# One converted weight per two units in the second gated pass, and four re-ordered stretches around it

## The chip, the cores and the metric
The kernel runs on one core of one Trainium2 chip. The metric is the time of one execution on the device in microseconds (us): lower is better. Three runs of the kernel before gave 1425.16 us as their median (1423.47 to 1425.9). Differences of under 0.2% (some 2.9 us) can't be told from none here.

## The reference, cut to what matters
Eight batches and eight heads of an attention between 512 tokens and 32 state rows (64 wide), read both ways, then a gated layer over the 4352 rows, then a second layer with a piecewise quadratic activation. All is float32.

```python
# attention, per batch and head: x is 512x64, state is 32x64
a     = softmax(scale * x @ state.T);   xread = a @ state      # 512x64
a2    = softmax(scale * state @ x.T);   sread = a2 @ x         # 32x64
x = concat(xread, sread) over rows, heads side by side -> (8*544, 512)
# layer 1 (w_gate, w_val 512x1536; w_out 1536x512)
x = (sigmoid(x @ w_gate) * (x @ w_val)) @ w_out
# layer 2 (w_in 512x2048; w_out 2048x512): g is 0, (h+1)^2/4 or h by where h lies
h = x @ w_in
out = where(h >= 1, h, where(h <= -1, 0, (h+1)**2/4)) @ w_out
```

## The kernel before, in words
Each float32 product is made of three products of shortened halves (high times high, high times low, low times high), so every operand is split: ScalarE (ACT) copies the high half, VectorE (DVE) subtracts it to get the low half. The program is one long order written out by hand: each engine works through its own queue in order, and a wait at the head of a queue holds all that is behind it. SyncE (SP) issues nearly all DMAs, in order as well.

The stages, in order of time:

- **First attention** (0 to 50 us), for batches 0 to 3, order in the string `PRE`. Each word is a step with a number: `X` transposes x on TensorE (PE) and ACT copies it; `st`/`sb` do that for the state; `S` scores, `E` their copy, `A` their transpose, `m` maximum and subtraction on DVE, `x` exp on ACT, `n` normalisation (`att_n`), `T` transpose with the high half on ACT, `L` the low half on DVE; `p` and `j` (`Weights.parts`, `Weights.join`) convert one weight tile, two instructions on ACT, then two on DVE; `M` multiplies a pair of weights by the state (PE, then the high half on ACT), `K` is its low half on DVE; `Q` begins the first gated products. In `att_n` the sum over 32 columns is made by halving adds on GpSimd (POOL), two small DVE instructions follow, and POOL multiplies. 14 transposes of the identity run ahead of the first data (L1366).
- **First gated pass** `gated(0)` (to 215 us), 24 units, a unit being 24 products of 128x512.
- **First output pass** `output1(0)` (to 378 us): 24 units of four slots each (`slot1(n, k)`, n from 0 to 95); a slot is six products of 128x512. The second half's attention and the state-side reads are items placed at slot numbers by hand: `t_item` (T of the second half) at 36, 38, 58, 60, `att_n` of the last head pair at 56, `sr_e` (a maximum on DVE, two exps on ACT, then five small DVE instructions) at 49, 51, 53, 55 for the second half, `sr_items` at 62 to 88. At slot 70 four weight tiles `wa` are loaded.
- **Second gated pass** `gated(1)` (to 543 us). In each unit PE does half of its products, `prev()` evacuates the unit before (two sigmoids on ACT, L658, or two multiplies on DVE, L661), one pair of `m_item` may follow, then `split_ws` splits a weight tile into a two-buffered tile `w` and stores it, and `parts`/`join` convert weights for layer 2; an even unit has two rounds of `split_ws` and `parts`, an odd one two joins. `more_wa` loads the next `wa` tiles as far as splits and products allow. `m_pair` of an odd unit needs the PSUM tiles that the two sigmoids empty.
- **Second output pass** `output1(1)` (to 734 us), again slots (`slot2`). From slot 0 on, every second slot does one step of `wi_steps`, which load, combine, split and store the eight weight blocks of layer 2; the state rows `xs` are split at slot 5; at slot 71 the four loads of the third `ws` block are issued, out of space that the steps' tiles held. After slot 71 `state_block` does layer 1 for the state rows, then the slots 72 to 95 take one step each of the list `early`: four loads of y, four loads of weights, sums, high and low halves.
- **Layer 2** (to the end), with its steps planned at tick numbers. `to_last` plans the first operands of the last products.

The lines that decide are these, of `gated`:

```python
else:                                # bg == 1
    for _ in range(2):
        if i % 2 == 0 or i == 1:
            split_ws()
        if i % 2 == 0:
            if len(weights.first) < 2:
                weights.parts()
        elif i > 1:
            weights.join()
```

Of the kernel before, what the change touches and what calls it, by code (L numbers as in the profile page):

```python
# [25 lines left out]
def attention_moe_moe_kernel(  # L26
# [28 lines left out]
    nc = tc.nc  # L55
# [277 lines left out]
        t = t_of(bg, hp)  # L333
        nc.scalar.activation(out=t, in_=t, func=AF.Exp, scale=SCALE)

    def att_n(bg, hp, eng=None):
        t = t_of(bg, hp)
        u = att.tile([128, 16, 2, 1], F32, tag="u", name="u", bufs=2)
        if eng:
            v = att.tile([128, 16, 2, N // 2], F32, tag="v", name="v", bufs=1)  # L340
            n = N // 2
            src = t
            while n:
                o = v[:, :, :, :n] if n > 1 else u
                eng.tensor_tensor(
                    out=o, in0=src[:, :, :, :n], in1=src[:, :, :, n : 2 * n], op=ALU.add
                )
                src, n = v, n // 2
        else:
            nc.vector.tensor_reduce(out=u, in_=t, axis=AX.X, op=ALU.add)  # L350
        nc.vector.tensor_scalar(out=u, in0=u, scalar1=1e-9, scalar2=None, op0=ALU.add)
        nc.vector.reciprocal(out=u, in_=u)
        (eng or nc.vector).tensor_tensor(
            out=t, in0=t, in1=u.to_broadcast([128, 16, 2, N]), op=ALU.mult
        )
# [242 lines left out]
    def gated(bg, begun=None, hooks={}):  # L598


        sg_t = {}
        prev = None
        for i in range(4 * NQ):
            q, mm, v = i // 4, i // 2 % 2, i % 2
            if i == 0 and begun:
                ps = begun
            else:
                ps = [ps_tile(v) for _ in range(2)]
                if i == 0:
                    quads(ps, bg, q, mm, v, [((0,), 0)])  # L610
                    for _ in range(2):
                        m_item(1)
                    quads(ps, bg, q, mm, v, [((0,), 1)])
                    split_ws()
                else:
                    quads(ps, bg, q, mm, v, [((0, 1), 0)])
                if prev:
                    prev()
                if (i in (2, 3) or i > 4 and i % 2) if bg else i % 2:
                    for _ in range(2):  # L620
                        if m_done[bg] < 4 * NQ:
                            m_item(1 - v)
            if bg == 0:
                flush()
                weights.low()
                weights.high()
                weights.join()
                weights.load()
                weights.parts()
                if i % 2 == 0 and i < 18:  # L630
                    weights.parts()
                    weights.join()
            else:
                for _ in range(2):
                    if i % 2 == 0 or i == 1:
                        split_ws()
                    if i % 2 == 0:
                        if len(weights.first) < 2:
                            weights.parts()
                    elif i > 1:  # L640
                        weights.join()
            flush()
            weights.load()
            if i in hooks:
                hooks[i]()
            if i:
                quads(ps, bg, q, mm, v, [((0, 1), 1)])
            elif not begun:
                quads(ps, bg, q, mm, v, [((1,), 0), ((1,), 1)])
            if bg:  # L650
                more_wa()

            def evac(q=q, mm=mm, v=v, ps=ps):
                m = 2 * q + mm
                for t in range(2):
                    if v == 0:
                        sg_t[t] = sgp.tile([128, 2, 512], F32, tag="sg", name="sg", bufs=4)
                        nc.scalar.activation(out=sg_t[t], in_=ps[t], func=AF.Sigmoid)  # L658
                    else:
                        sg = sg_t[t]  # L660
                        nc.vector.tensor_tensor(out=sg, in0=sg, in1=ps[t], op=ALU.mult)  # L661
                        stores.append(
                            lambda sg=sg, t=t: nc.sync.dma_start(
                                out=h_dram[bg][:, m, 2 * t : 2 * t + 2], in_=sg
                            )
                        )

            prev = evac
        prev()
        flush()  # L670
# [621 lines left out]
    def combine(j, b, k, acc, cs, ev):  # L1292
# [55 lines left out]


    PRE = (  # L1350
# [3 lines left out]
    ).split()  # L1354
    st_r = load_state(0, nc.sync)
    weights.todo += [job_m(i) for i in range(8)]
# [6 lines left out]
    weights.load(1)  # L1363
    make_identity(nc, ident)
    warm = ps_tile(1)
    for i in range(14):  # L1366
        nc.tensor.transpose(warm[:, i % 2, :128], ident, ident)
    nc.vector.memset(half, 0.5)
    for b in range(4):
# [7 lines left out]
    for w in PRE:  # L1377
# [18 lines left out]
        elif c == "E":  # L1396
            att_e(0, n)
        elif c == "n":
            att_n(0, n, nc.gpsimd)
        elif c == "T":  # L1400
            att_t(0, n // 2, n % 2, 1)
        elif c == "L":
# [127 lines left out]
    for i, n in enumerate((18, 28, 40, 50)):  # L1530
        place(n, s_item(i))
        place(n + 2, a_item(i))
    for i, n in enumerate((36, 38, 58, 60)):
        place(n, t_item(i // 2, i % 2))
    place(56, lambda k: att_n(1, HP - 1))
    for i, n in enumerate((5, 7, 13, 21)):
        place(n, lambda k, i=i: sr_e(0, i))
    for i, n in enumerate((49, 51, 53, 55)):
        place(n, lambda k, i=i: sr_e(1, i))
    for f, n in zip(sr_items(0), (11, 13, 15, 17, 19, 21, 23, 27, 29, 31, 33, 35, 37)):  # L1540
        place(n, f)
    for f, n in zip(sr_items(1), (62, 64, 66, 68, 70, 74, 76, 78, 80, 82, 84, 86, 88)):
        place(n, f)

    def slot1(n, k):
# [21 lines left out]
            weights.slot()  # L1567
        if n == 90:
            m_item(k)
        if n == 94:  # L1570
            nc.scalar.activation(out=table, in_=half, func=AF.Sigmoid)

# [14 lines left out]
    mp = pool("mp1", side="right", stack=st_a)  # L1587
    sgp = pool("sgp1", side="right", stack=st_a)
    m_item(0)
    gated(1, None, {14: lambda: load_h(4, 0), 18: lambda: load_h(4, 1)})  # L1590
    while wsq:
        split_ws()
# [26 lines left out]
    early, lows = [], []  # L1619

    def slot2(n, k):
        if n == 5:
            nc.scalar.activation(out=xs_hi, in_=f32(xs_lo), func=AF.Copy)
            tt(nc.vector, xs_lo, f32(xs_lo), f32(xs_hi))
        if 8 <= n < 72 and n % 8 == 0:
            load_ws((n - 8) // 32, (n - 8) // 8 % 4)
        if n < 70:
            if n % 2 == 0 and wi_steps:
                wi_steps.pop(0)()
        elif n == 70:  # L1630
            st_g.close()
            wsps.append(pool("wsp2", stack=st_g))
        elif n < 72:
            for j in range(4):
                load_ws(2, j)
        elif early:
            early.pop(0)()

    def state_block(b):
# [28 lines left out]
        h3 = splits_y(0, range(7), nc.vector)[:3]  # L1668
        yh = [lambda f=f: lows.append(f()) for f in h3]
        yl = lambda: lows.pop(0)()  # L1670
        early.extend([*loads, *ld[:3], sums[0], ld[3], sums[1], wh[0], wl[0], sums[2], wh[1]])
        early.extend([wl[1], sums[3], wh[2], wl[2], wh[3], wl[3], yh[0]])
        early.extend([lambda: (yh[1](), yl()), lambda: (yh[2](), yl()), yl])

    output1(1, slot2, state_block)
# [108 lines left out]
    def to_last():  # L1784
# [2 lines left out]
        htp = pool("htp", side="right")  # L1787
        S0 = prep_h(0)
        for i, f in enumerate(f for s in sorted(S0) for f in S0[s]):
            plan(start[9] + 3 + 2 * i // 3, f)  # L1790

    plan(start[9], to_last)
    t = 0
# [67 lines left out]
```

## Time and profile before

| what | value |
|---|---|
| median of three runs | 1425.16 us |
| the profiled execution itself | 1424.11 us |
| its span, first to last instruction | 1422.3 us |
| PE busy | 1377.1 us, 97% |
| DVE, ACT, POOL busy | 889.9, 741.9, 278.6 us |
| mean granted clock of PE | 0.992 |
| mean DMA rate | 221 GB/s |

PE is busy nearly all the time. The 45.2 us in which it is not, and the stretches in which its granted clock is at the lower of its two levels (1.2 in place of 2.4 GHz), are what an order of instructions can change. A granted clock of 1.00 is the upper level, 0.50 the lower.

### The profile page before, as it was taken

Reading aid. Unit: us, or ns where it says so; the run is one execution under the profiler, and the core shown is the slowest. Engines: PE = TensorE matmul, PEld = TensorE weight load, DVE = VectorE, ACT = ScalarE, POOL = GpSimd, SP = SyncE. Lnnn points to the kernel's source line nnn. Section 1 sums busy time; section 2 is a strip of 40 time slices with the busy share of each in tenths; the row PEclk is TensorE's granted clock in tenths of the full one; section 3 lists DMA queues with packets and bytes.
Section 4 is the critical chain, followed back from the end, with each engine's and each line's share of the span. In section 5 each row is a group of like instructions: output and inputs, shape, how many; then the busy total and the mean of one; then the engine's idle time right before and its main releaser. Section 6 shows DMA issues by size and latency. Waiting matters only on the chain. (4 is left out here: it accounts for less than half of the span.)

```text
span 1422.3 us, 23220 instructions
## 1 busy us (share of the span) xinstructions
PE 1377.1 (97%) x9022; PEld 1166.6 (82%) x9022; DVE 889.9 (63%) x1289; ACT 741.9 (52%) x1097; POOL 278.6 (20%) x179
## 2 busy tenths in 40 slices
PE   7899999989989999999999999999999999999997
PEld 5677787777756677889978888878879999999997
DVE  5766566585356544542286665666578978787775
ACT  6655556564444432322267777787775434343432
POOL 4200000000000000000018867698823100000000
PEclk9999999999999999999999999999999999999999
DMA  7577786959577755989266558866458343433332
GB/s 237 181 255 258 262 295 227 300 191 323 189 266 266 273 217 192 356 324 346 96 227 238 194 199 291 328 237 240 168 198 330 119 149 120 148 123 122 120 127 89
DMA packets 152798, 313.74 MB, mean 221 GB/s; under 512 B 14192, under 2 KB 81776, under 8 KB 151280
## 3 DMA queue, kind: packets, MB, share of 16 engines
q1 hardware_dynamic: 151880, 311.48, 62.8%
q8 instruction: 71, 1.16, 0.3%
q10 hardware_dynamic: 808, 0.79, 0.2%
q14 instruction: 39, 0.32, 0.1%
HBM read 182.58 MB, written 129.63 MB: 220 GB/s over the span
## 5 line engine op out<-in xcount | busy, mean ns | idle before, releaser
L1100 PE MATMUL u<-yc,wt 128*128 128x512 f32 x1344 | 306.8, 390 | 2.3 <-ACT m L1108 1.2
L1100 PEld LDWEIGHTS u<-yc,wt 128*128 128x128 f32 x1344 | 251.7, 188 | 56.6 <-ACT m L1108 2.3
L590 PE MATMUL ps<-at_hi,M 128*128 128x512 f32 x768 | 243.9, 394 | 0.0
L590 PEld LDWEIGHTS ps<-at_hi,M 128*128 128x128 f32 x768 | 144.6, 188 | 49.1 <-issue 19.3
L835 POOL TENSOR_TENSOR w2c<-w2c 128x256 f32<-128x256 f32 (+2 forms) x38 | 36.2, 966 | 700.1 <-DMA w2c<-w_dram 695.2
L590 PE MATMUL ps<-at_lo,M 128*128 128x512 f32 x384 | 150.0, 391 | 0.8 <-DVE at_lo L377 0.8
L745 PE MATMUL ps<-oh_lo,wo 128*128 128x512 f32 x368 | 145.6, 396 | 4.2 <-DVE oh_lo L713 4.2
L744 PE MATMUL ps<-oh_hi,wo 128*128 128x512 f32 x368 | 149.4, 406 | 0.0
L746 PE MATMUL ps<-oh_hi,wo 128*128 128x512 f32 x368 | 144.9, 394 | 0.0
L1169 PE MATMUL o<-w,hc 128*128 128x256 f32 x476 | 135.1, 284 | 1.5 <-POOL w L835 1.4
L1168 PE MATMUL o<-wt,hc 128*128 128x256 f32 x476 | 135.0, 284 | 1.4 <-DVE cu L1298 0.7
L1170 PE MATMUL o<-wt,hc 128*128 128x256 f32 x476 | 134.8, 283 | 0.3 <-DVE hc L1216 0.3
L1170 PE MATMUL o<-w,hc 128*128 128x256 f32 x476 | 134.8, 283 | 0.0
L1169 PE MATMUL o<-wt,hc 128*128 128x256 f32 x476 | 134.7, 283 | 0.0
L1168 PE MATMUL o<-w,hc 128*128 128x256 f32 x476 | 134.7, 283 | 0.0
L1212 ACT ACTIVATE hc<-hc 128x512 fp32r<-128x512 f32 (+1 forms) x108 | 64.8, 602 | 125.1 <-DMA hc<-hd_dram 112.9
L575 DVE TENSOR_TENSOR M<-ps,M 128x1024 fp32r<-128x1024 f32 x48 | 56.6, 1218 | 107.1 <-ACT M L569 107.1
L1022 POOL TENSOR_TENSOR yc<-yr,yc 128x1024 fp32r<-128x1024 f32 x49 | 116.6, 2424 | 5.3 <-ACT yc L1019 5.3
L1060 DVE SCALAR_TENSOR_TENSOR sg<-u,sg 128x512 f32<-128x512 f32 x96 | 66.2, 691 | 73.2 <-ACT u L1059 72.2
L1212 ACT ACTIVATE hc<-hs 128x512 fp32r<-128x512 f32 (+1 forms) x144 | 80.0, 598 | 58.3 <-DVE hs L1209 58.3
L1058 ACT ACTIVATE u<-sg,half 128x512 f32<-128x512 f32 x96 | 66.4, 692 | 67.6 <-DVE sg L1078 65.8
L1216 DVE TENSOR_TENSOR hc<-hs,hc 128x512 fp32r<-128x512 f32 (+1 forms) x144 | 93.0, 676 | 8.0 <-ACT hc L1212 7.8
(160 smaller groups left out, 2751.8 us busy)
## 6 DMA issues: line engine op xcount, KB each, us to landing
hd_dram<-sg SPq DMA_DIRECT2D x64, 512.0 KB, 5.0
h_dram<-sg SPq DMA_DIRECT2D x48, 512.0 KB, 4.2
oh_lo<-h_dram SPq DMA_DIRECT2D x48, 512.0 KB, 5.7
hc<-hd_dram SPq DMA_DIRECT2D x96, 256.0 KB, 4.1
yr<-y_dram SPq DMA_DIRECT2D x32, 512.0 KB, 6.7
wraw<-in_moe_w_out_dram SPq DMA_DIRECT2D x28, 512.0 KB, 6.0
ws_dram<-w SPq DMA_DIRECT2D x24, 512.0 KB, 5.6
ws<-ws_dram SPq DMA_DIRECT2D x24, 512.0 KB, 8.8
```

The costliest lines, as they stand in the source:

```text
L590: nc.tensor.matmul(out=ps[bp][:, b2], lhsT=M[:, l, b2, c], rhs=a[:, b2], start=(hq == 0 and j == 0), stop=(hq == 1 and j == 2),)
L744: nc.tensor.matmul(out=ps, lhsT=wh[:, c], rhs=hi, start=first, stop=False)
L745: nc.tensor.matmul(out=ps, lhsT=wh[:, c], rhs=lo, start=False, stop=False)
L746: nc.tensor.matmul(out=ps, lhsT=wl[:, c], rhs=hi, start=False, stop=last)
L1022: low_on.tensor_tensor(out=t[:, 1, :n], in0=src, in1=f32(t[:, 0, :n]), op=SUB)
L1058: nc.scalar.activation(out=s, in_=c, func=AF.Relu, bias=half, scale=0.5)
L1100: nc.tensor.matmul(out=pm[j], lhsT=a, rhs=b, start=not more and k == 0 and i == 0, stop=k == 1 and i == 2, skip_group_check=more,)
L1168: nc.tensor.matmul(out=ps, lhsT=wh, rhs=vh, start=start and i == 0, stop=False)
L1169: nc.tensor.matmul(out=ps, lhsT=wh, rhs=vl, start=False, stop=False)
L1170: nc.tensor.matmul(out=ps, lhsT=wl, rhs=vh, start=False, stop=last)
L1212: nc.scalar.activation(out=get(j)[0], in_=raw(j), func=AF.Copy)
L1216: nc.vector.tensor_tensor(out=lo, in0=raw(j), in1=f32(hi), op=SUB)
```

## The change
Six edits, none of which changes what is computed.

1. **First attention.** A new `PRE`; 23 warm transposes in place of 14; the halving adds on POOL are kept for head pairs 1 and 2 alone, pairs 0 and 3 sum with one DVE reduction. POOL multiplies in all four.
2. **Second gated pass.** An even unit does its two splits together and then one `parts`, an odd unit one `join`.
3. **Its start.** Two splits, with their stores, go into slots 92 and 93 of the output pass before, and `more_wa` is called once ahead of the pass.
4. **Items of the first output pass.** `sr_e` of the second half at slots 25, 39, 45, 57; its last two T at 60 and 62; its `sr_items` at 64 to 92.
5. **Second output pass.** The steps for layer 2 begin at slot 6, the split of `xs` is at slot 10, and the list `early` has a new order.
6. **Layer 2.** In `to_last`, steps that fall on the second tick of a unit go one tick later.

```diff
-    def att_n(bg, hp, eng=None):
+    def att_n(bg, hp, eng=None, halves=False):
...
-        if eng:
+        if halves:
             v = att.tile([128, 16, 2, N // 2], F32, tag="v", name="v", bufs=1)
...
             else:
-                for _ in range(2):
-                    if i % 2 == 0 or i == 1:
-                        split_ws()
-                    if i % 2 == 0:
-                        if len(weights.first) < 2:
-                            weights.parts()
-                    elif i > 1:
-                        weights.join()
+                if i % 2 == 0 or i == 1:
+                    split_ws()
+                    split_ws()
+                if i % 2 == 0:
+                    if len(weights.first) < 2:
+                        weights.parts()
+                elif i > 1:
+                    weights.join()
...
     PRE = (
-        "X00 st sb X01 X10 S0 E0 X11 p0 A0 m0 S1 E1 X20 x0 A1 X21 j0 p1 S2 E2 m1 x1 j1 p2 A2 n0 m2 "
-        "X31 j2 X30 n1 M0 S3 E3 x2 p3 A3 M1 K0 T0 m3 n2 K1 L0 j3 p4 x3 T1 Q0 p5 L1 M2 M3 n3 Q1 K2 K3 "
-        "T2 j4 L2 T3 Q2 L3 Q3 j5 g"
+        "X00 X01 st sb X10 p0 S0 E0 X11 p1 A0 S1 E1 X20 j0 X21 m0 j1 p2 A1 m1 M0 j2 S2 E2 x1 K0 A2 "
+        "p3 m2 X30 j3 n1 X31 x0 M1 S3 E3 M2 n0 K1 K2 A3 x2 m3 p4 T0 L0 x3 n2 T1 n3 Q0 p5 L1 M3 K3 "
+        "Q1 j4 T2 T3 L2 L3 Q2 j5 Q3 g"
...
-    for i in range(14):
+    for i in range(23):
...
-            att_n(0, n, nc.gpsimd)
+            att_n(0, n, nc.gpsimd, n in (1, 2))
...
-    for i, n in enumerate((36, 38, 58, 60)):
+    for i, n in enumerate((36, 38, 60, 62)):
...
-    for i, n in enumerate((49, 51, 53, 55)):
+    for i, n in enumerate((25, 39, 45, 57)):
...
-    for f, n in zip(sr_items(1), (62, 64, 66, 68, 70, 74, 76, 78, 80, 82, 84, 86, 88)):
+    for f, n in zip(sr_items(1), (64, 66, 68, 70, 74, 76, 78, 80, 82, 84, 86, 88, 92)):
...
+        if n in (92, 93):
+            split_ws()
+            flush()
...
     m_item(0)
+    more_wa()
     gated(1, None, {14: lambda: load_h(4, 0), 18: lambda: load_h(4, 1)})
...
-        if n == 5:
+        if n == 10:
             nc.scalar.activation(out=xs_hi, in_=f32(xs_lo), func=AF.Copy)
...
-            if n % 2 == 0 and wi_steps:
+            if n % 2 == 0 and n >= 6 and wi_steps:
...
-        early.extend([*loads, *ld[:3], sums[0], ld[3], sums[1], wh[0], wl[0], sums[2], wh[1]])
-        early.extend([wl[1], sums[3], wh[2], wl[2], wh[3], wl[3], yh[0]])
+        early.extend([*ld[:2], *loads, ld[2], wh[0], lambda: (wl[0](), ld[3]()), wh[1], wl[1]])
+        early.extend([lambda: None, *sums, wh[2], yh[0], wl[2], wh[3], wl[3]])
...
-            plan(start[9] + 3 + 2 * i // 3, f)
+            t = start[9] + 3 + 2 * i // 3
+            plan(t + (place[t][1] == 1), f)
```

## Rows read from the trace of the kernel before
**Rows 1.** The page: busy times, then the granted clock by fortieths of the span.
```profile
PE 1377.1 (97%) x9022; PEld 1166.6 (82%) x9022; DVE 889.9 (63%) x1289; ACT 741.9 (52%) x1097; POOL 278.6 (20%) x179
PEclk9999999999999999999999999999999999999999
```
**Rows 2.** Waits of PE: line, released by: us in total, times, longest.
```profile
PE ps L557 <- ACT sg L658: 6.3, 4, 1.7
PE ps L745 <- DVE oh_lo L713: 4.2, 4, 2.8
PE ps L557 <- DMA wa<-wf_dram: 2.8, 1, 2.8
```
**Rows 3.** Timeline of the second gated pass: start, us, instruction, [idle before, releaser].
```profile
419.12 0.66 ACT L158 ACTIVATE ca<-wraw 128x512 f32<-128x512 f32 x1 [5.28 <-DMA wraw<-in_moe_w_in_dram]
...
421.29 2.01 PE L557 MATMUL ps<-wa,sT 64*32 64x512 f32 x32 [1.57 <-ACT sg L658]
...
478.41 1.95 PE L557 MATMUL ps<-wa,sT 64*32 64x512 f32 x32
```
**Rows 4.** Timeline of that pass's first three units.
```profile
390.55 0.63 ACT L526 ACTIVATE w<-wa 128x512 fp32r<-128x512 f32 x1 [4.13 <-DMA ws_dram<-w]
...
392.82 1.85 SPq L514 DMA_DIRECT2D wa<-wf_dram  x3
...
398.30 1.93 PE L557 MATMUL ps<-wa,sT 64*32 64x512 f32 x24 [2.76 <-DMA wa<-wf_dram]
```
**Rows 5.** Timeline of output pass one, slots 49 to 60; then a window (clock follows POOL).
```profile
292.53 1.21 DVE L388 TENSOR_REDUCE m<-e 128x2 f32<-128x1024 f32 x1
...
310.18 1.23 DVE L353 TENSOR_TENSOR t<-t,u 128x1024 f32<-128x1024 f32 x1
...
311.55 1.94 PE L365 MATMUL ps<-ident,t 128*128 128x128 f32 x8 [3.86 <-DVE r L407]
...
312.00:316.00 4.00, 4.00 (x16) 3.49 (x16) 3.90 (x6) 2.15 (x3) 0.00 (x0) 0.66 0.02 4
```
**Rows 6.** Timeline of output pass two's start; then two windows.
```profile
546.24 1.33 SPq L705 DMA_DIRECT2D oh_lo<-h_dram  x2
...
547.62 2.19 SPq L854 DMA_DIRECT2D wg<-wir_dram  x4
...
553.44 1.06 ACT L711 ACTIVATE oh_hi<-oh_lo 128x1024 fp32r<-128x1024 f32 x1 [11.93 <-DMA oh_lo<-h_dram]
...
555.48 1.23 DVE L835 TENSOR_TENSOR xs_lo<-xs_lo,xs_hi 128x1024 fp32r<-128x1024 f32 x1 [7.89 <-ACT xs_hi L1623]
...
557.89 0.80 PE L745 MATMUL ps<-oh_lo,wo 128*128 128x512 f32 x1 [2.77 <-DVE oh_lo L713]
...
560.00:564.00 4.00, 4.00 (x11) 3.08 (x11) 1.74 (x2) 2.23 (x2) 0.00 (x0) 0.51 0.07 26
564.00:568.00 4.00, 4.00 (x19) 3.33 (x18) 2.05 (x2) 1.06 (x1) 0.00 (x0) 1.00 0.25 22
```
**Rows 7.** Timeline of output pass two after the state rows.
```profile
716.33 1.70 ACT L890 ACTIVATE wt<-wt 128x1792 fp32r<-128x1792 f32 x1 [4.69 <-DMA wt<-wi_dram]
```
**Rows 8.** Timeline of the first attention.
```profile
36.66 0.18 DVE L351 TENSOR_SCALAR u<-u 128x32 f32<-128x32 f32 x1 [1.82 <-POOL u L345]
...
38.37 1.97 PE L365 MATMUL ps<-ident,t 128*128 128x128 f32 x8 [3.85 <-DVE M L575]
...
43.84 1.92 POOL L353 TENSOR_TENSOR t<-t,u 128x1024 f32<-128x1024 f32 x1 [0.68 <-DVE u L352]
```
**Rows 9.** Timeline of SP and PE around slots 48 to 72 of pass two.
```profile
618.38 0.48 SPq L874 DMA_DIRECT2D wi_dram<-wg  x1
...
626.98 0.79 SPq L854 DMA_DIRECT2D wg<-wir_dram  x2
...
645.24 1.75 SPq L805 DMA_DIRECT2D ws<-ws_dram  x4
...
647.63 0.28 PE L216 MATMUL ps<-xs_hi,ws 128*128 128x256 f32 x1
```

## The prediction
> **What bounds the kernel now.** I read the page first. PE is busy 97% of the span and no other engine more than 63% [rows 1], so the end is set by PE's work and by the holes in it; the change touches no product, so only holes and slow clock can go. The granted clock has 9 in every fortieth, which hides short drops, so I looked in finer windows where PE waits. Second view: who PE waited for. Three rows carry 13.3 us [rows 2]: a product that needs PSUM tiles emptied by the sigmoids (6.3 us, four times 1.6), one that needs a weight tile from DMA (2.8 us, once), and the output passes' low halves (4.2 us, four times, one of them 2.8 us). Third view, the timeline at each hole, for what is late behind the engine that is named. The reader is to see that in most of them the named engine is busy with something else or stands behind a DMA: they are holes of order, not of load.
>
> **The change part by part.** I count each hole by its row, and the clock loss after it.
>
> *Second gated pass, one conversion per two units.* At 419.12 ACT stands 5.28 us for a weight block that was asked for in the unit just before; the sigmoids are queued behind it, and PE waits 1.57 us for them at 421.29 [rows 3]. That repeats every two units, four times in all, 6.3 us [rows 2]. Where no conversion is left, the same product starts without any idle time (478.41) [rows 3]. With two conversions per pair of units the second one uses a block loaded in the unit just before. With one, a block is loaded two odd units ahead, some 14 us, against 5.3 us that it took here. The ten conversions left then last until unit 20, the joins until 23, which is the end of the pass; ACT and DVE have the room (no unit has more than its two sigmoids or multiplies, two M halves, two splits and one conversion). Gain 6.3 us. If the cover is gone, each microsecond by which ACT waits beyond about 3.7 (5.28 less 1.57) is a microsecond of PE.
>
> *Its start.* Three splits in unit 0 share two buffers, so the third waits 4.13 us for a store (390.55); SP stands behind that split's store, and the next `wa` loads go out at 392.82, too late for the product at 398.30, which waits 2.76 us [rows 4]. After the change two splits are done in slots 92 and 93, unit 0 has two left for buffers whose stores left some slots before, and two `wa` loads are issued ahead of the pass. These loads wait at the head of SP's queue until the second product of the pass has freed their buffers; behind them stand only stores of unit 0. Gain 2.8 us. What is added in slots 92 and 93 is two copies on ACT of 0.63 us (the split at 390.55) [rows 4], two subtractions on DVE as long and two stores, beside products of PE; nothing of PE waits for it.
>
> *Items of the first output pass.* At 311.55 the T of slot 58 has waited 3.86 us; its data are ready when DVE ends the multiply that began at 310.18 [rows 5]. DVE is late because from 292.53 on four `sr_e`, each 1.21 us with small instructions behind it, were queued in slots 49 to 55 ahead of it. After the change one of the four stands near, at 57, behind `att_n` in the queue and not ahead of it, and T has two more slots. So the wait goes. PE ran at the lower level after it: 0.66 in the next 4 us, and the transposes at 311.55 took 1.94 us [rows 5]; 4 times 0.34 is 1.4, and 0.2 for the half microsecond before. Gain 3.9 + 1.6 = 5.5. What is late next: `sr_e` at 45 comes just ahead of the low half that slot 48 needs, behind `att_n` of slot 44; there I allow 0.3 us.
>
> *Second output pass, first slots.* The loads for the third unit are issued at 546.24, and four loads of layer 2's weights follow at once; all share the DMA engines, and the first lands only at 553.44. Then ACT splits, copies `xs`, and on DVE the subtraction of `xs` at 555.48 goes ahead of the low half, so PE waits 2.77 us at 557.89 [rows 6]. Until 564 it then runs at the lower level (0.51 and x11 against x19 products in 4 us) [rows 6]: from 557.89 that is 6.1 us at half speed, 3.0 lost. After the change nothing but stores and `xs` is ahead of that load, 2 MB in all in place of 3 (the four weight loads are 1 MB). What moved from 545.7 to 553.4 was these 3 MB; two thirds of 7.7 us is 5.1, landing at about 551, and ACT and DVE need 1.06 and 1.2 more: 553.3, against 555.1 (557.89 less 2.77), where PE begins to need it. Gain 2.8 + 3.0 = 5.8.
>
> *The list `early`.* The other waits for low halves in rows 2 are 4.2 - 2.8 = 1.4 us; all but 0.3 of it lies between slots 72 and 96, where ACT stands 4.69 us for a weight block (716.33) [rows 7] and DVE behind it. Now two blocks are loaded ahead of y, and sums come after the first two low halves. Gain 1.2, between 0 and 1.4.
>
> *First attention.* T1 waits 3.85 us at 38.37 for K1's DVE instruction, and K1 stands in DVE's queue behind the one at 36.66 that waits for POOL's sum of pair 2 [rows 8]. In the new order K1 and K2 are ahead of that sum, so this hole goes; what is late next is POOL itself, whose last multiply begins at 43.84 and ends at 45.76 [rows 8], ahead of T2 and T3. I put the new order down queue by queue, each instruction at the later of its engine's last end and its inputs, with the durations of the trace (the old order put down so comes within 0.4 us of where the trace has it): pair 2's sum on POOL 35.2 to 38.9, its multiply 39.6 to 41.5, pair 3's to 43.4, then T2 at 44.0. That is 45.8 - 43.4 = 2.3 us sooner. Bounds: two DVE reductions more, by the nearest row (1.21 us of 292.53) [rows 5], and two conversions ahead of the first E, up to 2.4 us lost; all of the 3.85 and 1.7 of slow clock after it, 5.5 gained. I take 2.3, the value that the walk gives. The nine more transposes end before the second half of the first x arrives: nothing.
>
> *Layer 2.* Two or three DVE instructions go one tick later, from ahead of the adds that empty PSUM to behind one of them; one 0.7 us instruction leaves the way of one wait. 0 to 1 us; I take 0.2.
>
> Sum: 6.3 + 2.8 + 5.5 + 5.8 + 1.2 + 2.3 + 0.2 = 24.1, less 0.3 is 23.8. From the profiled execution's own 1424.1 us that gives 1400.3, and the median of the runs stands 1.1 above it: 1401.4. I add half a microsecond for waits too small to be seen ahead: 1402.
>
> **The rivals.**
>
> *The tail of layer 2's loads.* A rule that speaks against beginning the loads six slots later is in the Trainium skill, DMA: Bandwidth & Descriptors, section Rules for kernel authors: issue a DMA early and wait for it late. The trace shows what it would do here: a store of the steps at 618.38 holds the next load until 626.98, 8.6 us, as they share a buffer; the last such store now leaves in slot 68, and the third `ws` block's loads (645.24, slot 71) need its space, so they can slip by up to 4 to 6 us. That block is needed behind 120 products of 256 columns that begin at 647.63 [rows 9]; at half of 4 us for 19 of 512 columns [rows 6] these take 12.6 us, to 660.2. Issued at 649 to 651 in 1.75 us and 7.2 us on the way like the load at 546.24 [rows 6], it lands between 658 and 660: some 0 to 2 us to spare. If they are used up, PE stands up to 6 us in the state rows, with its clock perhaps lower after it: +4 to +8, 1406 to 1410. For it: DMA is near full there. Against: the margin.
>
> *The first slots' hole stays.* If stores, `xs` and the reads fill the DMA engines until 553 without the weights too, slot 8 waits as before: +5.8, 1408. Against: the 1 MB that leaves.
>
> *The attention's hole moves.* The `sr_e` at 39 and 45 delay a low half, or DVE is still behind at slot 60: +5.5, 1407.5.
>
> *Slower than before: the conversions still stand behind their loads.* Place: ACT ahead of the sigmoids, now for nine conversions from unit 4 to 20 and no more for four. SP works in order; if a store of `w` or of h that stands ahead holds the weight load, each of the nine costs PE what it is late beyond 3.7 us. The other places gain 17.5; from 23.8 / 9 = 2.6 us of PE a time, so from a wait of 6.4 us on ACT, the change is slower; at 7.3 us it costs 9 x 3.6 = 32, 1433. For it: the same wait in rows 3 and more pairs that can have it. Against: the load is a pair of units earlier.
>
> **How the numbers follow.** The forecast has a chance of 0.60, the tail 0.12, the first slots 0.11, the attention 0.10, the late conversions 0.07 (0.04 of it slower, 0.03 near break-even). The forecast's own range is 1398 to 1406: first attention 5.5 for 2.3 on one side, 2.4 lost on the other. With any one of the first three rivals it reaches 1410; with the first attention's lower bound beside it 1413; below, 1396 if also the small items give their most. Range 1396 to 1413. A time within 0.2% of 1425.2, 2.9 us, can't be told from no change: faster 0.93, same 0.03, slower 0.04.
>
> **What would show it.** Right: no wait of PE for the sigmoids and no DMA wait of ACT ahead of them between 400 and 550; no idle PE ahead of the first product of unit 2; T at slot 60 without idle time; the granted clock at 1.00 in the two windows that had 0.66 and 0.51; T1 without a hole and the first gated products some 2 us sooner. Wrong: a wait of PE for `ws` in the state rows; the hole at slot 8; a row of waits for the sigmoids longer than four.

## The result, and the profile after

Four runs of the kernel after have a median of 1403.77 us (1402.56 to 1406.81), four of the kernel before, on the same chip, 1424.32 us (1421.89 to 1425.9). The ratio is 0.986, with a 95% interval of 0.9838 to 0.9883: 20.6 us gone, where 23.2 were forecast (1425.2 less 1402). The profiled execution took 1404.33 us, its span is 1402.5.

The page's busy row and clock row of the kernel after answer to [rows 1]: PE busy 1374.3 for 1377.1 us in a span 19.8 us shorter, so most of what went is idle time.

```profile
PE 1374.3 (98%) x9031; PEld 1166.7 (83%) x9031; DVE 892.2 (64%) x1291; ACT 740.9 (53%) x1097; POOL 270.6 (19%) x169
PEclk9999999999999999999999999999999999999999
```

The waits of PE in the kernel after (total, times, longest): the three rows of [rows 2] are gone. What leads now are the first attention (L308, L365, L590), a wait in layer 2 (L1100) that was 1.2 us before and is 3.1 now, and one in the last products (L1169) that was 1.4 and is 2.7.

```profile
PE ps L308 <- ACT e L292: 4.4, 4, 2.1
PE u L1100 <- ACT m L1108: 3.1, 3, 2.1
PE o L1169 <- POOL w L835: 2.7, 4, 0.7
PE ps L365 <- POOL t L353: 2.4, 1, 2.4
PE ps L590 <- DVE at_lo L377: 1.5, 2, 0.8
```

In the second gated pass's timeline after, the products of M in unit 2 (389.16) and unit 5 (409.68) start without idle time, as do the conversions of units 4 and 6 on ACT ([rows 4, 3]: 2.76 us at 398.30, 1.57 at 421.29, and 5.28 on ACT at 419.12); the second of these conversions uses the block that SP asked for at 403.04:

```profile
389.16 1.95 PE L557 MATMUL ps<-wa,sT 64*32 64x512 f32 x32
...
400.76 0.68 ACT L158 ACTIVATE ca<-wraw 128x512 f32<-128x512 f32 x1
...
403.04 0.43 SPq L148 DMA_DIRECT2D wraw<-in_moe_w_in_dram  x1
...
409.68 1.95 PE L557 MATMUL ps<-wa,sT 64*32 64x512 f32 x32
...
413.74 0.66 ACT L158 ACTIVATE ca<-wraw 128x512 f32<-128x512 f32 x1
```

The late T of the first output pass follows on DVE's multiply without a wait, and `sr_e` stands behind that multiply ([rows 5]: 3.86 us):

```profile
306.06 1.23 DVE L353 TENSOR_TENSOR t<-t,u 128x1024 f32<-128x1024 f32 x1
307.20 1.21 DVE L388 TENSOR_REDUCE m<-e 128x2 f32<-128x1024 f32 x1
309.57 1.03 PE L365 MATMUL ps<-ident,t 128*128 128x128 f32 x8
```

Windows of the kernel after around that T and at the second output pass's slots 8 to 10 (the column before the last two is the granted clock) have 1.00 where [rows 5, 6] had 0.66 and 0.51; in the timeline below them `xs` on DVE comes behind the low halves and no longer ahead of them:

```profile
306.00:310.00 4.00, 4.00 (x21) 3.33 (x20) 3.93 (x6) 1.50 (x4) 0.00 (x0) 1.00 0.83 295
...
539.00:543.00 4.00, 4.00 (x19) 3.30 (x19) 3.70 (x6) 1.12 (x2) 0.00 (x0) 1.00 0.94 287
```
```profile
534.87 1.06 ACT L711 ACTIVATE oh_hi<-oh_lo 128x1024 fp32r<-128x1024 f32 x1 [10.17 <-DMA oh_lo<-h_dram]
...
535.97 1.23 DVE L713 TENSOR_TENSOR oh_lo<-oh_lo,oh_hi 128x1024 fp32r<-128x1024 f32 x1 [5.19 <-ACT oh_hi L711]
...
540.35 1.22 DVE L835 TENSOR_TENSOR xs_lo<-xs_lo,xs_hi 128x1024 fp32r<-128x1024 f32 x1
```

To see where the time went I cut PE's timeline at the starts of a few instructions: the first product of Q2 that needs a low half (49.46 in before), the transposes of the second half's state (L240, 216.18), the product of M that runs just ahead of the second gated pass (378.49), the first product of the second output pass (L726), of the state rows (L216), of layer 2 (L1100), of the last products (L1168), and the last one. The stretch between the first two of these cuts lies between the first two columns and takes 166.6 to 167.1 us in every kernel. It holds the first gated pass and the first 18 us of the first output pass, which begins at 198.25 in the trace of before and not at 215. All kernels of the experiments stand in the table, one profiled execution each, in us:

| kernel | first attention | output pass 1 | gated pass 2 | first slots to state rows | state rows, `early` | layer 2's units | last products |
|---|---|---|---|---|---|---|---|
| before | 49.46 | 162.31 | 165.35 | 103.79 | 86.27 | 331.59 | 347.89 |
| only_pace | 49.05 | 162.29 | 158.18 | 102.15 | 85.78 | 332.27 | 349.74 |
| only_start | 48.84 | 162.61 | 162.43 | 102.63 | 86.33 | 332.16 | 347.66 |
| only_items | 49.22 | 157.52 | 167.19 | 101.99 | 85.73 | 334.84 | 348.18 |
| loads6 | 48.25 | 162.17 | 164.59 | 102.36 | 85.72 | 334.09 | 350.30 |
| xs10 | 48.87 | 162.97 | 165.50 | 99.48 | 86.91 | 332.58 | 349.25 |
| after | 48.31 | 157.30 | 154.86 | 97.92 | 84.50 | 334.96 | 349.31 |
| after_l0 | 48.27 | 157.28 | 154.85 | 98.26 | 84.50 | 335.28 | 348.89 |
| after_xs5 | 47.24 | 157.43 | 154.85 | 99.56 | 84.50 | 334.87 | 349.88 |
| no_shift | 47.95 | 157.20 | 154.85 | 97.92 | 84.50 | 331.97 | 347.87 |
| lows_first | 46.10 | 157.22 | 154.86 | 98.04 | 84.50 | 330.92 | 349.51 |
| best | 47.87 | 157.24 | 154.86 | 97.92 | 84.50 | 330.16 | 349.04 |
| best_conv | 46.92 | 157.28 | 154.85 | 97.92 | 84.50 | 330.16 | 348.84 |

Before against after: 1.15, 5.01, 10.49, 5.87 and 1.77 us gained, 0.16 in the stretch with the first gated pass, 3.37 lost in layer 2's units and 1.42 in the last products: 19.66. A column of kernels that share their code there shows what one execution can tell: the first attention differs by 1.2 us among six kernels that have the old order, layer 2's units by 3.25 among the six with the old layer 2.

### The profile page after: what moved, and what is told of

It is laid out like the page before. It is cut to its first block, busy times and chain, and to the rows that moved or that the text cites. A ratio compares the mean times of both kernels' runs of the same rounds, so it can differ in the third digit from the quotient of the medians.

```text
span 1402.5 us, 23243 instructions
## 1 busy us (share of the span) xinstructions
PE 1374.3 (98%) x9031; PEld 1166.7 (83%) x9031; DVE 892.2 (64%) x1291; ACT 740.9 (53%) x1097; POOL 270.6 (19%) x169
## 5 line engine op out<-in xcount | busy, mean ns | idle before, releaser
L1100 PE MATMUL u<-yc,wt 128*128 128x512 f32 x1344 | 308.5, 391 | 3.9 <-ACT m L1108 3.1
L1100 PEld LDWEIGHTS u<-yc,wt 128*128 128x128 f32 x1344 | 252.8, 189 | 58.8 <-ACT m L1108 4.3
L590 PE MATMUL ps<-at_hi,M 128*128 128x512 f32 x768 | 244.3, 394 | 0.1
L590 PEld LDWEIGHTS ps<-at_hi,M 128*128 128x128 f32 x768 | 144.7, 188 | 50.0 <-issue 19.3
L590 PE MATMUL ps<-at_lo,M 128*128 128x512 f32 x384 | 150.4, 392 | 1.5 <-DVE at_lo L377 1.5
L1169 PE MATMUL o<-w,hc 128*128 128x256 f32 x476 | 135.2, 284 | 2.7 <-POOL w L835 2.7
L1168 PE MATMUL o<-wt,hc 128*128 128x256 f32 x476 | 135.0, 284 | 1.4 <-DVE cu L1298 0.7
L1169 PE MATMUL o<-wt,hc 128*128 128x256 f32 x476 | 134.7, 283 | 0.0
L1168 PE MATMUL o<-w,hc 128*128 128x256 f32 x476 | 134.7, 283 | 0.0
L711 ACT ACTIVATE oh_hi<-oh_lo 128x1024 fp32r<-128x1024 f32 x48 | 50.6, 1056 | 92.9 <-PE ps L746 59.1
```

The costliest lines, as they stand in the source:

```text
L590: nc.tensor.matmul(out=ps[bp][:, b2], lhsT=M[:, l, b2, c], rhs=a[:, b2], start=(hq == 0 and j == 0), stop=(hq == 1 and j == 2),)
L1100: nc.tensor.matmul(out=pm[j], lhsT=a, rhs=b, start=not more and k == 0 and i == 0, stop=k == 1 and i == 2, skip_group_check=more,)
L1168: nc.tensor.matmul(out=ps, lhsT=wh, rhs=vh, start=start and i == 0, stop=False)
L1169: nc.tensor.matmul(out=ps, lhsT=wh, rhs=vl, start=False, stop=False)
```

## The experiments

**The pace alone.**

```diff
+                if i % 2 == 0 or i == 1:
+                    split_ws()
+                    split_ws()
+                if i % 2 == 0:
+                    if len(weights.first) < 2:
+                        weights.parts()
+                elif i > 1:
+                    weights.join()
```


> The kernel before with edit 2 alone: in the second gated pass an even unit does one pair of splits and one conversion, an odd unit one join. Theory (a conversion that uses a block asked for one unit before is what holds the sigmoids): the four waits of PE for the sigmoids go, the stretch from the first M product ahead of the pass (378.5 in the trace of before) to the first product of output pass two (543.8) gets 6.3 us shorter, the idle 2.8 us ahead of the first product of unit 2 stays, nothing else moves: about 1418. Rival (the sigmoids are late because ACT has too much to do, or the wait goes with the pass's start, edit 3): the waits stay, fewer or shorter by under 2 us in all, and the time is 1422 to 1425. Rival of the slower side (the conversions still stand behind their loads): a row of more than four waits, 1425 to 1433.

1417.77 us in one run beside 1421.77 of before. The four waits are gone from the list of PE's waits, 2.2 us ahead of the products of M in unit 2 stay, and the pass takes 158.18 in place of 165.35: 7.2 us. The theory holds.

**The start alone.** Only the two splits in slots 92 and 93 and the one `more_wa`.

```diff
+        if n in (92, 93):
+            split_ws()
+            flush()
...
     m_item(0)
+    more_wa()
```


> The kernel before with edit 3 alone: two splits with their stores in slots 92 and 93 of the first output pass, more_wa once ahead of the second gated pass. Theory: the idle PE ahead of the first product of unit 2 (2.1 to 2.8 us in five runs of kernels without this edit) goes, the second gated pass gets 2.8 to 3.5 us shorter, 165.4 to some 162; the four waits for the sigmoids stay at 6.2 us in all; no wait comes in the last slots of the pass before. Rival (the hole belongs to the two splits per round, edit 2, and only moves to a later unit): a wait of PE for wa or for the sigmoids of 1.5 us or more in another unit, and a gain of under 1.5 us.

1420.29 us. The wait for `wa` is gone and the pass takes 162.43, 2.9 us less than before; the waits for the sigmoids stay. In PE's waits of this kernel they are even longer than the 6.3 us of [rows 2]:

```profile
PE ps L557 <- ACT sg L658: 7.0, 4, 1.8
```

7.2 and 2.9 are 10.1 of the 10.5 that both give together.

**The items alone.**

```diff
-    for i, n in enumerate((36, 38, 58, 60)):
+    for i, n in enumerate((36, 38, 60, 62)):
...
-    for i, n in enumerate((49, 51, 53, 55)):
+    for i, n in enumerate((25, 39, 45, 57)):
```
(and `sr_items` from 64 on)

> The kernel before with edit 4 alone: sr_e of the second half at slots 25, 39, 45, 57, its last two T at 60 and 62, its sr_items from 64. Theory: the 3.9 us of idle PE at slot 58 go and the granted clock there is 1.00 in place of 0.66, so the first output pass (216.2 to 378.5 in the trace of before) gets 5 us shorter, 1419 in all. Rival (the hole moves to a low half behind the sr_e at 39 or 45, or DVE is still behind at slot 60): a new wait of 2 us or more in the pass and a gain of 0 to 2 us.

The output pass takes 157.52 in place of 162.31, as expected, and no wait of over 0.72 us is left in it. But the time of the run was 1422.58 beside 1421.77 of before: layer 2's units, where nothing is changed, took 3.25 us more than in the trace of before, the second gated pass 1.8. By its one time this edit would have been called worthless.

**The two halves of the second output pass's start.**

```diff
# loads6
-            if n % 2 == 0 and wi_steps:
+            if n % 2 == 0 and n >= 6 and wi_steps:
# xs10
-        if n == 5:
+        if n == 10:
             nc.scalar.activation(out=xs_hi, in_=f32(xs_lo), func=AF.Copy)
```


> The kernel before with one half of edit 5's start: the steps for layer 2 begin at slot 6, the split of xs stays at slot 5. Theory of the prediction (the 1 MB of weight loads pushes back the third unit's load, by about 2.4 us): that load lands at about 551 on the clock of before, the hole of 2.8 us at 557.9 goes and with it the stretch at the lower clock, 5.8 us in all, 1418. Rival (the subtraction of xs on DVE, ahead of the low half, is what decides): the load lands sooner but the hole stays at 1.2 us or more, the gain is under 3 us.

> The kernel before with the other half of edit 5's start: the split of xs at slot 10, the weight loads from slot 0 as they were. Theory of the prediction: the third unit's load still lands late, at about 553.4 on the clock of before, then ACT needs 1.06 and DVE 1.2 us, so PE still waits for the low half, by 0.6 us or a little more, without the 1.23 us of the subtraction and the copy; whether a hole of that length brings the lower clock is open: the gain is 2 us if it does as before, 5 us if it does not. Rival (xs decides alone): no hole at all and the clock at 1.00, 5.8 us gained. Rival (the loads decide alone): the hole stays at 2 us or more and nothing is gained.

1424.61 and 1422.96 us in one run each, beside 1421.77 of before: by these times neither gains anything, so what follows goes by the stage. In the timeline of loads6 the load lands 9.34 us after the pass began (541.63), as before (9.60) and as in three kernels that have both halves as before (9.25, 9.54, 9.07). The first weight load behind it goes out 6.0 us after the pass began in place of 3.8, and two of them (256 KB each) in place of five before it lands; that moved it by no more than these kernels differ. `xs` is still ahead of the low half:

```profile
550.97 1.06 ACT L711 ACTIVATE oh_hi<-oh_lo 128x1024 fp32r<-128x1024 f32 x1 [11.67 <-DMA oh_lo<-h_dram]
...
555.43 0.70 PE L745 MATMUL ps<-oh_lo,wo 128*128 128x512 f32 x1 [2.53 <-DVE oh_lo L713]
```

In that of xs10 it lands as late (9.41), and PE waits 0.5 us, with the clock at 1.00 in the windows behind:

```profile
553.39 1.06 ACT L711 ACTIVATE oh_hi<-oh_lo 128x1024 fp32r<-128x1024 f32 x1 [11.73 <-DMA oh_lo<-h_dram]
...
555.76 0.50 PE L745 MATMUL ps<-oh_lo,wo 128*128 128x512 f32 x1 [0.51 <-DVE oh_lo L713]
```

So `xs` decides, not the loads: the rival of loads6 was right. In xs10 the half microsecond that the load still costs is there as expected.

The same from the other side, each half undone in the kernel after:

> The kernel after with one half of edit 5 undone: the steps for layer 2 begin at slot 0 again, xs stays at slot 10. In the kernel before with the xs half alone the third unit's load landed 9.4 us after the pass began, as in the kernel before (9.6), and PE's hole was 0.5 us in place of 2.8; with the loads half alone it landed at 9.3 and the hole was 2.5. In the kernel after it landed at 7.8. Theory (the order of DVE decides, and the sooner landing comes from the pass before, which ends with fewer DMAs): it lands at about 7.8 again, no hole, the stretch from the pass's start to the state rows within 0.5 us of the 97.9 of the kernel after. Rival (the weight loads do push the load back once the pass before leaves room for it): it lands at 9.2 or later, a hole of 0.5 us comes back, the stretch is 1 to 1.6 us longer.

> The kernel after with the other half of edit 5's start undone: xs is split at slot 5 again, the weight loads begin at slot 6. Theory (xs, 2.0 us of ACT and DVE ahead of the low half, decides; the loads do not): the third unit's load lands 7.6 to 8.7 us after the pass began as in the kernels after, PE needs its low half at 11.3; 2.3 us for the two halves and 2.0 for xs make 11.9 to 13.0: a hole of 0.7 to 1.7 us comes back, the stretch to the state rows is 98.6 to 100 in place of 97.9. Rival (with the weight loads away xs no longer matters): no hole, 97.9 to 98.1.

With the loads from slot 0 again (1404.76 us) there is no hole and the stretch takes 98.26 for 97.92: that half is worth 0.3 us at most. With `xs` at slot 5 again (1405.51 us) 1.34 us of hole come back, and 99.56. In all these kernels the load landed at 7.6 to 8.7; in the six that have one edit or none, at 9.1 to 9.6. Which of the edits together bring it forward no run tells apart.

**Is it edit 6 that layer 2 lost by?**

```diff
-            t = start[9] + 3 + 2 * i // 3
-            plan(t + (place[t][1] == 1), f)
+            plan(start[9] + 3 + 2 * i // 3, f)
```


> The kernel after without edit 6, the shift in to_last. Layer 2's units took 331.6 us before, 335.0 after, and 332.3, 334.8, 334.1 and 332.6 in four kernels whose layer 2 is that of before. Theory (the loss comes from a wait of POOL for y, whose length varies, and not from this edit): the wait of PE for ACT's m after unit 22 is again 0.9 to 2.8 us, with the clock below 1.00 behind it where it is near 2 us or more; in the last units a wait of 1.1 for sg and one of 0.3 to 0.4 for m (1.4 in all) stand in place of the four with 1.8 in all; time within 1 us of the kernel after, apart from the first wait. Rival (edit 6 cost the 3.4 us): layer 2's units back at 331.6 whatever the first wait is, 1401 in all.

1400.08 us; 331.97 for layer 2's units. By these totals alone the rival would have won. But the first wait was 1.28 us this time, with the clock at 1.00 behind it: that, and not the edit, puts this kernel 2.2 us ahead of the kernel after by the start of the last units, and at their end it is 3.0 ahead. So edit 6 costs 0.8 us, of which 0.35 are waits that the profile lists (1.45 us in two for 1.80 in four). The kernels lows_first and best of the table, which have no first wait and differ in layer 2's units by edit 6 alone, say the same: 330.92 and 330.16. Of the 3.37 us that the units lost, 2.6 are left for the first wait: 1.2 of longer waiting and 1.4 of lower clock behind it. That wait can be read in ten kernels. In all of them SP issues the first of the four loads of y 166.6 us after layer 2's first product (166.57 to 166.59); what differs is when POOL can begin the sum, which needs the second and the third (us from that product):

| kernel | y's sum begins | wait of PE | granted clock, next 4 us |
|---|---|---|---|
| before | 180.85 | 0.90 | 1.00 |
| no_shift | 181.25 | 1.28 | 1.00 |
| only_start | 181.44 | 1.47 | 1.00 |
| only_pace | 181.54 | 1.57 | 1.00 |
| xs10 | 181.84 | 1.88 | 1.00 |
| loads6 | 181.89 | 1.93 | 0.67 |
| after | 182.06 | 2.10 | 0.61 |
| after_xs5 | 182.06 | 2.07 | 0.58 |
| after_l0 | 182.39 | 2.41 | 0.57 |
| only_items | 182.71 | 2.74 | 0.57 |

Each tenth of a microsecond by which the sum begins later is a tenth of waiting. In the five kernels at the end of the table the lower clock behind it is added: against before, layer 2's units lost 1.3 to 1.5 us more than their longer waits and, in the three that have it, edit 6 (loads6: 2.5 lost, 1.03 of it the wait). The trace of before has the shortest such wait of the ten. Whether the change makes it longer is open: in the kernel after and the three built on it SP issues the second of these loads 168.7 to 169.1 us after layer 2's first product, in the six others 168.4; but the sum begins at 181.25 to 182.39 in those four and at 180.85 to 182.71 in the six.

**The wait removed.** In the timeline of the kernel after, POOL stands 11.42 us for y; behind the first sum are two low halves of a weight block (4.2 us), though all that they need was done on ACT at 887.2; the other sums follow, and ACT's copy of one of them holds the activations:

```profile
885.45 1.70 ACT L930 ACTIVATE w2c<-w2c 128x1792 fp32r<-128x1792 f32 x1
891.51 2.41 POOL L835 TENSOR_TENSOR yr<-yr 128x1024 f32<-128x1024 f32 x1 [11.42 <-DMA yr<-y_dram]
893.87 4.22 POOL L835 TENSOR_TENSOR w2c<-w2c 128x1024 fp32r<-128x1024 f32 x2
898.03 7.13 POOL L835 TENSOR_TENSOR yr<-yr 128x1024 f32<-128x1024 f32 x3
900.47 1.06 ACT L1019 ACTIVATE yc<-yr 128x1024 fp32r<-128x1024 f32 x1 [4.44 <-POOL yr L835]
...
909.57 0.73 PE L1100 MATMUL u<-yc,wt 128*128 128x512 f32 x2 [2.10 <-ACT m L1108]
```
```diff
-            plan(t + 9, low[0])
-            plan(t + 10, low[1])
+            at.setdefault(t + 9, [])[:0] = low
```


> The kernel after with one more edit in layer 2: the low halves of the three split w2 blocks on POOL go ahead of the first y sum that is planned for the same tick. In the kernel after POOL stands 11.4 us for y at 891.5, while ACT's high half, all that the lows need, is done at 887.2; the two lows (4.2 us) run only behind the first sum, the other sums behind them, and ACT's copy of the second sum (4.4 us idle at 900.5) holds the activations for which PE waits 2.1 us at 909.6, with the clock at 0.61 in the next 4 us. Theory (POOL's order behind that DMA is what costs layer 2 its time): that wait goes, the clock stays at 1.00, layer 2's units take 331.5 or less in place of 335.0, 1400 to 1401.5 in all against 1403.8. Rival (the time is lost elsewhere, or the lows push the sums back where y lands early): layer 2's units stay at 333 or more, no difference in time.

1399.1 us (1398.5 to 1399.93, five runs; ratio to before 0.9818, 0.9804 to 0.9831). Layer 2's units take 330.92. In its timeline the lows fill POOL's wait, no sum of y stands for DMA, ACT's copy waits 0.44 us, and PE not at all:

```profile
885.24 4.22 POOL L835 TENSOR_TENSOR w2c<-w2c 128x1024 fp32r<-128x1024 f32 x2 [7.13 <-ACT w2c L930]
889.54 9.64 POOL L835 TENSOR_TENSOR yr<-yr 128x1024 f32<-128x1024 f32 x4
...
894.48 1.06 ACT L1019 ACTIVATE yc<-yr 128x1024 fp32r<-128x1024 f32 x1 [0.44 <-POOL yr L835]
```

The theory holds. Part of the 4.7 us against the kernel after is the first attention, which this time ended 2.2 us sooner with the same code.

**The last products and edit 6 together.**

```diff
-    for i, at_ in ((6, 32), (7, 39)):
+    for i, at_ in ((6, 28), (7, 35)):
```
(with the lows first, and without edit 6)

> The kernel after with the lows ahead of y's first sum (1399.1 in five runs by itself), without edit 6, and with the splits of the last two w2 blocks on ACT and POOL at steps 28 and 35 of the last products in place of 32 and 39. Theory for edit 6 (it spends 0.35 us in the last units): waits of 1.45 there in place of 1.79, layer 2's units 330.5 in place of 330.9. Theory for the splits (PE stands up to four times 0.7 us for POOL's low halves because they begin too late): these waits go, the last products take 347.0 or less in place of 347.7 to 350.3; in all 1396.5 to 1398. Rival (POOL slows DVE's low halves of h, which then are late): the waits for POOL are replaced by waits for DVE's hc, no difference within 1 us: 1398.5 to 1399.5.

1398.04 us (1396.53 to 1400.11, five runs). Layer 2's units: 330.16 (330.5 expected). The last products: 349.04, and the rival is right. In PE's waits the row for POOL is gone and one for DVE, 3.9 us, has come:

```profile
PE o L1170 <- DVE hc L1216: 3.9, 6, 1.5
```

In its timeline the DVE subtraction of 128x512 takes 0.69 us alone and 1.40 to 1.79 beside POOL's:

```profile
1064.81 5.84 POOL L835 TENSOR_TENSOR w<-w 128x512 fp32r<-128x512 f32 x4 [16.65 <-ACT w L958]
1065.26 1.40 DVE L1209 TENSOR_TENSOR hs<-ht,hc 128x512 f32<-128x512 f32 x1 [2.66 <-DMA hc<-hd_dram]
1066.68 1.66 DVE L1209 TENSOR_TENSOR hs<-hs,hc 128x512 f32<-128x512 f32 x1
1068.27 1.79 DVE L1209 TENSOR_TENSOR hs<-hc,ht 128x512 f32<-128x512 f32 x1
...
1079.87 0.69 DVE L1209 TENSOR_TENSOR hs<-hs,hc 128x512 f32<-128x512 f32 x1
```

The Trainium skill, GPSIMD Engine Reference, Specifications, says that POOL shares its SBUF interfaces with VectorE and contends with DVE instructions of two SBUF inputs; the trace agrees, with these 0.69 and 1.40 to 1.79 us. Four steps earlier moved POOL's 12 us onto other subtractions of DVE, for which PE then waits.

**The first attention.**

```diff
-        "X00 X01 st sb X10 p0 S0 E0 X11 p1 A0 S1 E1 X20 j0 X21 m0 j1 p2 A1 m1 M0 j2 S2 E2 x1 K0 A2 "
+        "X00 X01 st sb X10 S0 E0 X11 p0 A0 S1 E1 X20 p1 j0 X21 m0 j1 p2 A1 m1 M0 j2 S2 E2 x1 K0 A2 "
```


> The same kernel with one edit more in the first attention's order: the first two conversions (p0, p1) behind E0 and X11, and behind X20, and no longer ahead of E0 and E1. In the kernel after ACT stands 0.6 us for the first weight's load at 13.0 and then converts, 1.1 us; E0 begins at 14.1 and A0 on PE at 15.2, 2.1 us idle, with the clock at 0.83 in that tenth of microseconds in three of four kernels with this order. Theory (the conversions ahead of E are what keeps the new order's gain at 1.15 to 1.5 us of the 2.3 forecast): A0's hole is 0.5 us or so, the first attention ends 1 to 2 us sooner (46.1 to 48.3 in four kernels), the time falls by 1 to 2 us against the kernel beside it. Rival (POOL's chain, DVE and the loads of x set the end): the hole at A0 goes and the next ones, at A1 or T0, grow by as much: no difference within 0.7 us.

1397.25 us (1396.42 to 1397.99, four runs; ratio to before 0.9808, 0.9795 to 0.9822). A0's hole is 0.32 us in place of 2.13. But PE then stands 1.46 us for a load of x:

```profile
13.19 1.09 PE L308 MATMUL ps<-ident,e 128*128 128x128 f32 x8 [0.32 <-ACT e L292]
...
17.79 1.30 PE L265 MATMUL ps<-ident,xa 128*128 128x128 f32 x8 [1.46 <-DMA xa<-in_x_dram]
```

In all, from 9 us on PE waits 8.9 us in the stage where the kernel beside it waits 9.0, as the rival had it, which named the loads of x. What is gone is the lower clock behind A0 (1.00 from 14 to 18, 0.63 in the kernel beside it). The stage takes 46.92 in place of 47.87, but six kernels with one order there differ by 2.2 (46.10 to 48.31), and the times are 0.8 us apart with overlapping runs: that this edit gains anything is not shown. The version has the lowest median measured, and its interval lies below that of the kernel after.

## Why the prediction was right, point by point

*Pace and start of the second gated pass* (6.3 and 2.8 of the sum): 10.5 us together, 7.2 and 2.9 alone. Mechanism and place as said; the slower rival, conversions behind their loads, did not show: none of the nine conversions from 400.76 to 504.60 waits for a DMA. Two sizes were off. The cover is smaller than I said: a block is asked for 10.7 us ahead of its conversion (403.04 to 413.74), not some 14. And the sum counted the waits alone. Behind each of the four for the sigmoids a pair of units took 0.1 us longer, and the products of M behind the wait for `wa` took 2.76 us where they take 1.95 elsewhere; these make 1.3 of the 1.4 us by which the gain is larger.

*Items* (5.5 less 0.3): 5.0 in the pair of traces, 4.8 alone. No low half came late.

*First slots* (5.8): 5.87 in the pair of traces, but the step that argued it failed. It said that the 1 MB of weight loads pushed the load back and that 2 MB would land two thirds as late, at 551. The load did not move with them (9.34 for 9.60; 8.2 with the weight loads from slot 0 in the kernel after, 7.6 to 8.7 without). Of my step only the part on DVE's order was right: `xs` ahead of the low half. The 2.8 us of hole and 3.0 of clock were also the longest case; kernels with the same code there took 102.0 to 102.6 in place of 103.79, so the change is worth some 4 to 6.

*The list `early`* (1.2, between 0 and 1.4): 1.77, and 84.50 in every kernel that has it, against 85.7 to 86.9.

*First attention* (2.3): the mis-sized term, 1.15 in the pair of traces and 1.3 by the means of six kernels with the old order (48.95) and six with the new (47.62, best_conv left out). The reading was generous by itself: the walk has T2 at 44.0 and before has it at 45.96, which is 2.0. T1's hole of 3.85 us went, but T0, which now runs together with T1, waits 2.44 us for POOL where it waited 1.18, and A0 waits 2.12 us for E0 behind the conversions, where it did not wait at all; the walk, going to POOL's chain, did not price them on PE. In all, PE's waits in the stage from 9 us on fell by 1.6 us. POOL's last multiply ended at 43.91, where my walk had 43.4. And the walk ran at the upper clock: from 40 to 50 us of the kernel after the granted clock is 0.83, PE is still at the products of Q1 when POOL ends, and T2 begins at 44.87, 1.0 us behind it. How the rest divides among these no run shows.

```profile
15.18 1.09 PE L308 MATMUL ps<-ident,e 128*128 128x128 f32 x8 [2.12 <-ACT e L292]
...
35.34 2.47 PE L365 MATMUL ps<-ident,t 128*128 128x128 f32 x16 [2.44 <-POOL t L353]
...
42.00 1.91 POOL L353 TENSOR_TENSOR t<-t,u 128x1024 f32<-128x1024 f32 x1 [0.57 <-DVE u L352]
...
44.87 2.07 PE L365 MATMUL ps<-ident,t 128*128 128x128 f32 x16
```
```profile
40.00:50.00 10.00, 9.13 (x50) 5.39 (x49) 8.24 (x10) 6.01 (x9) 3.34 (x2) 0.83 0.22 75
```

*Layer 2* (0.2 gained): 3.37 lost in its units and 1.42 in the last products. The step failed in its sign: edit 6 itself costs 0.8 in the last units, where I forecast a gain. The other 2.6 are a wait for DMA, with the lower clock behind it, that was already in the trace of before, at its shortest there, and that I read as one of the small ones. The last products vary by 2.6 us among the six kernels with the old layer 2 (347.66 to 350.30), so their 1.42 says nothing.

The tail of layer 2's loads in the state rows did not show (no wait of PE in the 84.50 us); nor did the first slots' hole stay or the attention's hole move. Of the 23.8 us of the sum the pair of profiled executions shows 19.8 (1424.11 less 1404.33): 1.15 less in the first attention, 3.6 in layer 2's units and 1.4 in the last products, 1.4 more in the second gated pass and 0.6 in `early`. The median came 1.8 us above the forecast; that it came so near is in part luck: the first slots gave their 5.9 although the step that argued them failed, and the gated pass gave 1.4 more than its term while layer 2's units and the first attention took 4.7 away.

## What to carry to other kernels

An order written by hand is read queue by queue: find the instruction behind which the late one stands, and move that, not the load that seems to be late. What one run of an edit of 5 us tells can be undone by a wait elsewhere that varies by 3; cut PE's timeline into stages and compare each stage among all kernels that share its code. Where an engine stands for a DMA while its next work is ready, put that work ahead of the wait: here that one edit took layer 2's units from 334.96 to 330.92.

## What the runs showed of the hardware

- The four loads of y in layer 2, the first issued at the same point of the program in ten executions, held the sum behind them until 14.3 to 16.1 us later; from issue to landing the last of the four took 12.1 us in before, 14.1 in only_items. The Trainium skill, DMA: Bandwidth & Descriptors, Rules for kernel authors, wants DMAs issued early and waited for late; here some 14 us ahead was not early enough, and no run issued them earlier.
- Holes of like length did not always bring the lower clock. The 2.76 us of [rows 4] left it at 1.00 in the trace of before, where 2.77 us brought 0.51 [rows 6]; at A0 a hole of 2.12 us stands in a window with 0.83 in the kernel after, and one of 2.15 in a window with 1.00 in lows_first. At the place of [rows 4] itself, 2.05 us brought 0.57 over 397 to 401 in xs10. Why is open. Nor is a 1.00 of the records the whole story: in before the 32 products right behind the hole of [rows 4], which shows 24 of them, took 2.76 us, where the same products take 1.95 without one.

```profile
398.30 2.76 PE L557 MATMUL ps<-wa,sT 64*32 64x512 f32 x32 [2.76 <-DMA wa<-wf_dram]
398.00:402.00 4.00, 3.70 (x36) 1.48 (x37) 0.67 (x1) 1.73 (x2) 0.00 (x0) 1.00 0.93 366
```
- A load's landing changed little with the weight loads issued behind it on the same queue: 9.34 us with two of them behind it, from 6.0 us on (loads6), 9.07 to 9.60 with five of them, from 3.8 to 4.2 us on, in the five kernels that have them there.
